# Where four small weight sums stand in VectorE's queue: the first cross product quad of a gate/up stage

## The chip, the cores and the metric

One core of one Trainium2 chip runs the whole program. The metric is the device time of one execution in microseconds; medians of several executions are quoted. Every execution comes with the mean clock that was granted to TensorE (1.0 is full speed).

## The reference

A block of a transformer: layer norm, linear attention with 32 heads, a residual, a second layer norm, a gated ReLU feed-forward layer and a second residual. The change lies in the gate/up part of the feed-forward layer:

```python
# x: 1 x 2048 x 1024 bf16, W_gate and W_up: 1024 x 3584, W_down: 3584 x 1024
gate = jnp.einsum("bsd,df->bsf", x, W_gate)
up   = jnp.einsum("bsd,df->bsf", x, W_up)
gate = gate * (gate > 0)
h    = gate * up
return jnp.einsum("bsf,fd->bsd", h, W_down)
```

## The kernel before

All large products are computed with a fast 2 x 2 block scheme of seven block products, m1 to m7, in place of eight. It needs sums of blocks on both sides. VectorE makes them. One "quad" is one such scheme for 128 gate and 128 up columns of each of the two halves of the feed-forward layer (that is what the seven products combine) and one half of the tokens. Its weight sums (t1 to t4) are made ahead of it by four steps for gate and four for up:

```python
steps = [  # L693, L697, L698, L699; each 128 x 512, 16 bit
    first,                                                    # t1 = b12 - b11
    lambda: tt(out=t2, in0=b22, in1=t1, op=ALU.subtract),     # (shortened)
    lambda: tt(out=t3, in0=b22, in1=b12, op=ALU.subtract),
    lambda: tt(out=t4, in0=b21, in1=t2, op=ALU.subtract),
]
# products 1..7 take the weights  b11, b21, b22, t4, t1, t2, t3
```

The first four quads take one half of the tokens each ("single-token quads"). After them come groups of quads for both halves, and each group opens with a quad that also computes a "cross product", p1 to p7, the same scheme once more on a smaller block. Its weight sums are eight steps (L984, 128 x 256, gate and up in turn for t1, t2, t3, t4). In the names below, g0 to g3 are adds on VectorE with a ReLU on ScalarE behind them, x0 to x3 the products gate times up, j the joins of cross products (VectorE), and c and s copies (ScalarE). The "filling work" is sums for the later down product, with their stores.

In the traces of this case VectorE runs its instructions in the order in which the code emits them: the prediction derives the times of 16 starts from the code, and the changed kernel's trace has them in that order, each 0.1 us earlier. The matmuls of TensorE keep the order of the code too (in the trace of before p1 starts at 326.04, p2 at 326.90, m4 at 327.76, m3 at 330.73, p6 at 332.46, p5 at 333.32, m1 at 334.18, p7 at 335.91, m5 at 336.77, m6 at 338.63), while weight loads run ahead (the first of m6 by 0.34 us in the same trace). Work that is not urgent waits in a list, and `slot(n)` emits a share of it at fixed places between the urgent steps. The end of the last single-token quad, and the filling of the list at the head of each quad:

```python
# in the last single-token quad (r == NE - 1)
now = sums_of_run(r + 1)
steps = [p for pair in zip(*[steps for steps, _ in now]) for p in pair]   # t1 gate, t1 up, t2 gate, ...
work += cross_sums + cross_weight_sums(runs[r + 1][0]) + steps[:2]
held_back = steps[2:]
...
# at the head of every quad
work += held_back + later[:take]
held_back = []
...
if k:
    want = -(-len(fill) // max(nwin - 2 - k, 1))
    for p in range(want):
        work.insert(min(len(work), 2 * p + 1), fill.pop(0))    # filling work goes in between
```

The first cross quad, in order of emission and shortened ("prv" is the last single-token quad, whose final products run into this one):

```python
x["p1"](); x["c1"]()
prv["g3"]()          # VectorE: read accY (m5 + ...) and add: L925
x["p2"](); x["j00"]()
prv["m4"]()
slot(0, 9)
prv["x3"]()
prv["m3"]()          # TensorE: adds onto accY, so g3 must have read it
prv["rg"](); prv["x2"]()
x["p6"](); x["c2"](); x["p5"]()
prv["g1"](); slot(1, 8); prv["x1"]()
cur["m1"](); x["p7"](); x["c3"]()
cur["g0"]()          # VectorE: read accA
slot(2, 4)
cur["m5"](); x["j11"](); slot(3)
cur["m6"]()          # TensorE: adds onto accA; its weights are the t2 sums (L697)
...
```

## Time and profile before

| | before |
|---|---|
| time, median of 3 (lowest to highest) | 729.22 us (729.22 to 730.75) |
| span of the profiled execution | 727.5 us |
| TensorE busy | 719.0 us, 99% |
| VectorE busy | 583.2 us, 80% |
| TensorE's only wait in the gate/up stage (waits view) | 1.1 us, for the add g3 |

The page of a profile gives totals; the waits view gives, for each engine, whom it waited for and for how long; the timeline gives instructions in order of time, like ones merged. The prediction below shows the lines of all of these. One more reading is used throughout: the length of the first cross quad by starts, from its first matmul (p1) to the first matmul of the next quad (m1). A difference of two starts on the same engine doesn't depend on how the profile models the end of a matmul, nor on how late the whole program began.

```profile
326.04 0.59 PE L1004 MATMUL accA<-hn,wg 128*128 128x512 bf16 x2
...
343.81 1.03 PE L916 MATMUL accA<-hn,wg 128*128 128x512 bf16 x4
```

These are the two ends in the timeline of before, so the quad takes 343.81 - 326.04 = 17.77 us.

### The profile page before, as it was taken

To read this page: it belongs to the slowest core of one execution; us is meant where nothing else is said; L and a number is where in the kernel's file an instruction comes from. 1 tells how busy PE (TensorE), PEld (TensorE's weight loads), DVE (VectorE), ACT (ScalarE), POOL (GpSimd) and SP (SyncE) were. 2 spreads that over 40 slices of the span, in tenths; PEclk is the share of its full clock that TensorE was granted. 3 is DMA by queue.
4 is the path that set the end of the run, shared out by engine and by line. 5 is a ranking of instruction groups with operands and counts; after the bars stand their busy time and mean duration, and the time that the engine had idled before them with its cause. 6 is when DMAs were issued, how large, how long until landed. Compare 5 with 4: busy or idle time off the path is not lost.

```text
span 727.5 us, 10634 instructions
## 1 busy us (share of the span) xinstructions
PE 719.0 (99%) x4000; PEld 380.4 (52%) x4000; DVE 583.2 (80%) x1039; ACT 325.2 (45%) x580; POOL 20.8 (3%) x56
## 2 busy tenths in 40 slices
PE   8999999999999999999999999999999999999997
PEld 3454555444444444444444444444444468888666
DVE  6998754777898776889998998988977379996677
ACT  4786653878886564344444444443444120000000
POOL 1000000000000000000000000000000001100210
PEclk9999999999999999999999999999999999999999
DMA  9676003089986533197556585565653499977932
GB/s 318 166 139 174 0 1 115 3 181 232 229 174 170 132 79 109 49 276 210 174 176 195 200 257 202 186 189 179 211 163 128 151 394 313 326 263 261 260 45 59
DMA packets 144708, 128.89 MB, mean 177 GB/s; under 512 B 50960, under 2 KB 127888, under 8 KB 144656
## 3 DMA queue, kind: packets, MB, share of 16 engines
q1 hardware_dynamic: 137584, 123.30, 56.2%
q0 software_dynamic: 5312, 3.15, 3.5%
q10 hardware_dynamic: 1760, 1.77, 0.7%
q8 instruction: 31, 0.51, 0.3%
q14 instruction: 21, 0.17, 0.1%
HBM read 76.81 MB, written 39.85 MB: 160 GB/s over the span
## 4 chain that ended last, share of the span: by engine, by line
PE 92%; DVE 4%; ACT 2%; DMA 1%; issue 0%; SPq 0%; DVEq 0%; ACTq 0%
PE accA L916 21%; PE accA L1410 8%; PE attn L608 7%; PE Aq L365 6%; PE accX L916 6%; PE accY L916 5%; PE accA L1236 3%; PE Aq L789 3%; PE Aq L505 3%; PE accX L1410 3%; PE Eq L365 3%; PE accY L1410 3%; PE accA L1004 2%; PE vp L416 2%; PE kp L398 2%; PE Eq L789 2%
## 5 line engine op out<-in xcount | busy, mean ns | idle before, releaser
L921 ACT COPY snap<-accA 128x1024 f32<-128x1024 f32 x52 | 52.4, 1010 | 65.8 <-PE accA L916 65.6
L926 ACT ACTIVATE gu<-gu 128x512 bf16<-128x512 bf16 x72 | 45.4, 630 | 80.6 <-DVE gu L925 80.5
L916 PEld LDWEIGHTS <-tg 128*128 128x128 f16 x384 | 37.6, 98 | 45.4 <-issue 0.3
L916 PEld LDWEIGHTS <-tu 128*128 128x128 f16 x384 | 37.6, 98 | 45.3
L608 PE MATMUL attn<-wo_mem,oT 128*128 128x512 bf16 x256 | 59.0, 379 | 0.5 <-DVE o_sb L585 0.4
L916 PE MATMUL accA<-hn,tg 128*128 128x512 f16 (+1 forms) x192 | 49.3, 379 | 0.0
L916 PE MATMUL accA<-hn,tu 128*128 128x512 f16 (+1 forms) x192 | 49.3, 379 | 0.0
L205 ACT COPY u<-Aq 128x512 f32<-128x512 f32 x54 | 31.4, 581 | 36.5 <-PE Aq L365 19.7
L1410 PEld LDWEIGHTS <-x 128*128 128x128 f16 (+1 forms) x448 | 43.8, 98 | 5.5
L608 PEld LDWEIGHTS <-oT 128*128 128x128 bf16 x256 | 24.7, 98 | 29.9 <-issue 2.2
L925 DVE TENSOR_TENSOR gu<-accX,snap 128x1024 bf16<-128x1024 f32 x26 | 31.7, 1221 | 10.1 <-ACT snap L921 7.8
L925 DVE TENSOR_TENSOR gu<-accY,snap 128x1024 bf16<-128x1024 f32 x26 | 31.7, 1220 | 7.7 <-ACT snap L921 7.7
L916 PEld LDWEIGHTS <-wg 128*128 128x128 bf16 x208 | 20.3, 98 | 25.8 <-issue 1.4
L916 PEld LDWEIGHTS <-wu 128*128 128x128 bf16 x208 | 20.4, 98 | 24.5
L365 PEld LDWEIGHTS <-xT 128*128 128x128 bf16 (+1 forms) x192 | 18.6, 98 | 21.9 <-issue 0.3
L611 DVE SCALAR_TENSOR_TENSOR x_res<-attn,x_res 128x512 bf16<-128x512 f32 x32 | 22.0, 687 | 9.5 <-PE attn L608 9.3
L1374 POOL DMA_DIRECT2D out_dram<-o x12 | 15.2, 1265 | 502.7 <-DVE o L1370 501.0
L585 DVE TENSOR_TENSOR o_sb<-nd,rd 128x384 bf16<-128x384 f32 (+1 forms) x48 | 23.7, 509 | 7.1 <-ACT rd L584 6.1
L1410 PEld LDWEIGHTS <-xs 128*128 128x128 f16 x280 | 27.4, 98 | 3.2
L1416 DVE TENSOR_TENSOR snap<-accA,u 128x1024 f32<-128x1024 f32 x16 | 19.6, 1222 | 11.4 <-PE accA L1410 11.3
L929 DVE TENSOR_TENSOR hq<-gu 128x512 bf16<-128x512 bf16 x48 | 20.3, 423 | 10.0 <-ACT gu L926 9.8
L1236 PEld LDWEIGHTS <-x 128*128 128x128 bf16 (+1 forms) x168 | 16.4, 98 | 19.6
(268 smaller groups left out, 1516.7 us busy)
## 6 DMA issues: line engine op xcount, KB each, us to landing
x<-x_dram SPq DMA_DIRECT2D x17, 896.0 KB, 8.9
x_dram<-hq SPq DMA_DIRECT2D x28, 512.0 KB, 3.0
wg<-in_B_W_gate_dram SPq DMA_DIRECT2D x14, 512.0 KB, 4.6
wu<-in_B_W_up_dram SPq DMA_DIRECT2D x14, 512.0 KB, 5.8
x_dram<-hq SPq DMA_DIRECT2D x28, 256.0 KB, 2.4
wraw<-in_B_W_down_dram SPq DMA_DIRECT2D x14, 512.0 KB, 4.2
t_dram<-wt SPq DMA_DIRECT2D x21, 256.0 KB, 2.2
xd<-x_dram SPq DMA_DIRECT2D x6, 896.0 KB, 6.6
```

The costliest lines, as they stand in the source:

```text
L205: copies[nm, v] = nc.scalar.copy(out=snaps[nm, v], in_=bank[v][:])
L365: nc.tensor.matmul(ps[:], lhsT=left[m - 1][:, kc, r + v * P:r + (v + 1) * P], rhs=right[m - 1][:, kc, :], start=(start and kc == 0), stop= ...
L585: nc.vector.tensor_tensor(out=ov[:, c0:c0 + n], in0=ndv[:, :, 0:P].rearrange("p k (h e) -> p k h e", h=HPC), in1=rd[:, 0:n, :].unsqueeze(3 ...
L608: nc.tensor.matmul(ps[:], lhsT=st["oT"][:, c, :], rhs=wo_sb[:, c, j * NW:(j + 1) * NW], start=(c == 0), stop=(c == KC - 1))
L611: added[t, j] = nc.vector.scalar_tensor_tensor(out=h_sb[:, j * NW:(j + 1) * NW], in0=ps[:], scalar=1.0, in1=h_sb[:, j * NW:(j + 1) * NW], ...
L789: nc.tensor.matmul(ps[:], lhsT=w(v, m)[:, kc, :], rhs=left[m - 1][:, kc, :], start=(start and kc == 0), stop=(kc == KH - 1), skip_group_ch ...
L916: nc.tensor.matmul(ps[:, v, :], lhsT=w[v][n - 1][:, kc, :], rhs=left[n - 1][:, kc, :], start=(t is not None and kc == 0), stop=(kc == KH - ...
L921: nc.scalar.copy(out=st[nm][:], in_=halves(st["A"]))
L925: add(out=g[:], in0=halves(st[nm]), in1=st[base][:], op=ALU.add)
L926: nc.scalar.activation(out=g[:, 0, :], in_=g[:, 0, :], func=ACT.Relu)
L1236: nc.tensor.matmul(ps[:, t * NW:(t + 1) * NW], lhsT=x_tile(n, s, kh)[:, f, (t0 + t) * P:(t0 + t + 1) * P], rhs=w_tile(n, kh)[:, f, :], sta ...
L1410: nc.tensor.matmul(pv[:, tt, :], lhsT=left(m)[:, f, tt * P:(tt + 1) * P], rhs=right(m)[:, f, :], start=(t is not None and f == 0 and tt % ...
```

## The change

The intent: the cross product's last four weight sums are needed late (t3 for p7, t4 for p4), so they need not stand in front of the urgent add g3. They join the six sums that were already held back for the next quad, ten in all. This is called the first hunk below, though it stands last in the diff. The second hunk sends the filling work of that quad behind the held sums rather than between them.

```diff
-            held_back = []
...
                 for p in range(want):
-                    work.insert(min(len(work), 2 * p + 1), fill.pop(0))
+                    work.insert(len(work) if held_back else min(len(work), 2 * p + 1), fill.pop(0))
+            held_back = []
...
-                    work += cross_sums + cross_weight_sums(runs[r + 1][0]) + steps[:2]
-                    held_back = steps[2:]
+                    cross_steps = cross_weight_sums(runs[r + 1][0])
+                    work += cross_sums + cross_steps[:4] + steps[:2]
+                    held_back = cross_steps[4:] + steps[2:]
```

## The prediction

0.81 us won in front of g3, plus 0.13 us of waiting for g0, less 0.41 us lost anew at m6, came to 0.53 us.

> **What bounds the kernel now.** I read the page first: its header, the busy times and the slices.
>
> ```profile
> span 727.5 us, 10634 instructions
> PE 719.0 (99%) x4000; PEld 380.4 (52%) x4000; DVE 583.2 (80%) x1039; ACT 325.2 (45%) x580; POOL 20.8 (3%) x56
> PE   8999999999999999999999999999999999999997
> PEclk9999999999999999999999999999999999999999
> ```
>
> TensorE is busy for 719.0 of 727.5 us at full clock. No other engine can be the bound, and a change that removes no matmul can win at most 8.5 us, of which most lies at the two ends (the slices marked 8 and 7). Next I asked the waits view of TensorE, which says how much of those 8.5 us is waiting on another engine, and then the busy times by stretch through the stage that the change touches.
>
> ```profile
> PE tp L350 <- DVE xT L351: 1.4, 1, 1.4
> PE spin L451 <- DVE zero L448: 1.2, 1, 1.2
> PE accY L916 <- DVE gu L925: 1.1, 1, 1.1
> PE attn L608 <- DVE o_sb L585: 0.4, 1, 0.4
> ```
> ```profile
> 314.00:326.00 12.00, 12.00 (x57) 5.43 (x56) 10.32 (x20) 5.13 (x8) 0.00 (x0) 1.00 0.95 283
> 326.00:344.00 18.00, 16.92 (x78) 7.53 (x77) 17.30 (x38) 8.73 (x11) 0.00 (x0) 1.00 0.75 225
> 344.00:362.00 18.00, 18.00 (x85) 8.16 (x84) 16.26 (x32) 7.88 (x11) 0.00 (x0) 1.00 0.47 158
> 374.00:392.00 18.00, 18.00 (x85) 8.19 (x84) 14.99 (x28) 9.40 (x12) 0.00 (x0) 1.00 0.96 294
> ```
>
> The columns of the second fence are length, TensorE, weight loads, VectorE, ScalarE, GpSimd, clock, DMA. The stretch 326 to 344 us is the first cross product quad. It alone loses TensorE time (16.92 of 18.00), and there VectorE is busy 17.30 of 18.00 us, 96%. The next cross quad, 374 to 392, loses nothing. So the whole stage from 290 to 560 us has one gap, 1.1 us, and one owner. The timeline shows it (columns: start, duration, engine, line, output<-inputs):
>
> ```profile
> 328.39 0.28 DVE L984 TENSOR_TENSOR ct<-wg,ct 128x256 f16<-128x256 bf16 x1
> 328.59 0.29 DVE L984 TENSOR_TENSOR ct<-wu,ct 128x256 f16<-128x256 bf16 x1
> 328.63 1.03 PE L916 MATMUL accA<-hn,tu 128*128 128x512 bf16 x4
> 328.79 0.42 DVE L693 TENSOR_TENSOR tg<-wg 128x512 f16<-128x512 bf16 x1
> 329.12 0.42 DVE L693 TENSOR_TENSOR tu<-wu 128x512 f16<-128x512 bf16 x1
> 329.46 1.22 DVE L925 TENSOR_TENSOR gu<-accY,snap 128x1024 bf16<-128x1024 f32 x1
> 330.73 1.02 PE L916 MATMUL accY<-hs,wg 128*128 128x512 f16 x4 [1.08 <-DVE gu L925]
> 335.72 0.41 DVE L697 TENSOR_TENSOR tu<-wu,tu 128x512 f16<-128x512 bf16 x1
> 337.36 1.22 DVE L925 TENSOR_TENSOR gu<-accA,snap 128x1024 bf16<-128x1024 f32 x1
> 338.29 0.10 PEld L916 LDWEIGHTS <-tg 128*128 128x128 f16 x1
> 338.63 1.02 PE L916 MATMUL accA<-hs,tg 128*128 128x512 f16 x4
> ```
>
> The matmul at 330.73 is product m3 of the previous quad. It adds onto accY, which the vector add "g3" (L925) must first have read; g3 ran late, from 329.46 to 330.68, because it stood in VectorE's queue behind the weight sums of L984 and L693. Matmuls of this stage start every 0.86/4 = 0.215 us, so m3 could have begun at 328.63 + 0.86 = 329.49 and lost 1.24 us by starts (1.08 by modelled ends). The last lines show a second, small one: product m6 began at 338.63, not at 337.64 + 0.86 = 338.50, because "g0" ended at 338.58. Together 1.37 us by starts; nothing else in this stage is to be won.
>
> [...] 0.20 us for L984 (328.39 to 328.59), 0.33 for L693 (328.79 to 329.12), 1.13 for L925; the recorded durations, 0.29, 0.42 and 1.22, overlap by about 0.09. I use spacings, not durations. [...] m6's first load ran at 338.29, 0.34 us before its held matmul.
>
> **The change part by part.** It removes and adds no instruction; the order of TensorE and of ScalarE is the same, only VectorE's and the DMA queue's differ.
>
> Before, the last single-token quad queued eight sums for the cross product (L984) and two of the next quad's (L693), and six (L697, L698, L699 for gate and up) were held back to the first cross quad. Now the last four L984 sums are held back with those six: ten in the held list, but only four really move. In the new VectorE order these four no longer stand in front of g3: two come after it and after the join L1011, two after "g1". Removed in front of g3: 4 x 0.20 = 0.81 us (measured as the sum of those four spacings: 0.20, 0.20, 0.21, 0.20). The two instructions among them (a multiply and a sum, L929 and L759) move earlier; the multiply's input, a ReLU, was ready at 325.96 + 0.63 = 326.59, so nothing new waits.
>
> So g3 starts at 328.65 and ends at 329.87, and m3 follows 0.05 us later, as now, at 329.92: 0.81 us gained, 0.43 us of the gap kept.
>
> Now VectorE's chain to m6, with the spacings of today: join L1011 329.78; two moved sums 330.91 and 331.11; multiply 331.31; multiply from PSUM 331.65; three sums 332.37, 332.83, 333.17; g1 333.51 to 334.73; two moved sums 334.64 and 334.84; multiply at 335.48 (its ReLU ends at 335.45); sum 335.94; g0 336.28 to 337.50. TensorE wants m6 at 338.50 - 0.81 = 337.69, so g0 no longer holds it. But the moved sums push both L697 sums behind g0, and m6 has these as its weights. Gate's L697 runs 337.42 to 337.84. The wait now sits on the weight load, so 0.05 us for the signal and 0.21 us from load to matmul follow (as between 337.42 and 337.64): m6 at 338.10. That loses 0.41 us anew. Up's L697 ends at 338.17, before its loads at about 338.75.
>
> Sum at m6: 338.63 - 338.10 = 0.53 us. After it nothing should hold TensorE: the last moved sums lie before their products (L984's fourth sum at 335.13, product p4 at 339.82; join L1011 ends 339.96, p3 at 340.68). At 345.06 VectorE idles 0.88 us for a ScalarE copy, which itself follows TensorE, so the queue catches up there and the 0.53 us stay to the end, since later TensorE shows no wait. Predicted span 727.0 us, time 729.22 - 0.53 = 728.7 us.
>
> **The rivals.** First: the wait is wholly replaced, gain nothing, 729.2 us. The unbroken chain on VectorE between 335 and 338 us speaks for it: one more slip of half a microsecond in g1's ReLU or in the L697 sums and m6 gives all back. Against it: g1's and g0's spacings are those of the trace.
>
> Second: the wait at m6 is smaller than I think, because the loads are fetched during the running matmul. Then the gain is up to 0.81 + 0.13 = 0.94 us, 728.3 us. Against it: the load cannot start before its weights are written.
>
> Third: transfers. One filling sum (L759) goes from 332.06 to the end of the quad, about 343.3. Its store therefore leaves at about 343.8 instead of 332.51, and a load into the same buffer, which started at 339.17, must wait for that store to land (4.0 us in this stretch): to about 347.8, and lands about 7 us after, at 355. Its first reader is a vector sum in front of the store that the DMA queue issues at 370.29, so some 14 us remain. Only if that were an earlier reader (one at 350.5) would VectorE stop for several microseconds and TensorE lose perhaps 2 us: 731 us. I read the order of VectorE as showing the later one.
>
> Fourth: VectorE becomes the bound through the stage. The stretch 344 to 362 has it busy 16.26 of 18.00 us, so it has room, and the total of its work is unchanged.
>
> **Range and chances.** The known gap is 1.37 us, 0.19% of the time, so 2% (14.6 us) is out of reach upward, and downward only an unseen stop of many microseconds could do it. The three runs of before read 729.22, 729.22 and 730.75, so runs of one kernel differ by up to 1.5 us, more than the effect. Low end: the full 0.94 us and some luck, 727.5. High end: my 0.53 us on a run like 730.75, 730.3. Faster 0.01, same 0.98, slower 0.01.
>
> **What would show it.** In the waits view the entry accY L916 <- DVE gu L925 falls from 1.1 to about 0.3 us (0.43 by starts), and a new one of 0.2 to 0.4 us appears at accA L916, whose releaser is VectorE's L697, or as a gap in front of the weight load of tg. g3's add starts some 0.8 us nearer to the end of m4's matmuls. The cross quad ends 0.5 us sooner and TensorE's busy time in 326 to 344 rises by as much. I am wrong if g3 is still late (another instruction or a wait takes its place), if m6 loses over 0.9 us, or if a wait for the filling load shows on VectorE near 350 us.

## The result

| | before | changed |
|---|---|---|
| time, median of 6 | 729.43 us | 728.45 us |
| lowest to highest | 729.22 to 730.75 | 728.24 to 730.43 |
| span of the profiled execution | 727.5 us | 726.7 us |
| first cross quad by starts | 17.77 us | 17.03 us |

The ratio of the times is 0.9989, with a 95% interval from 0.9976 to 1.0002. A ratio here is the mean time of one kernel's runs over that of the other's of the same rounds, so it isn't quite the ratio of the medians in the table. The timer alone doesn't separate the two kernels; the trace does.

The waits view of TensorE after the change, against the one in the prediction (the columns are total, times, longest):

```profile
PE tp L350 <- DVE xT L351: 1.4, 1, 1.4
PE spin L451 <- DVE zero L448: 1.2, 1, 1.2
PE attn L608 <- DVE o_sb L585: 0.4, 1, 0.4
PE accY L916 <- DVE gu L925: 0.3, 1, 0.3
```

Nothing moved except the last line, from 1.1 to 0.3 us. The timeline shows both ends of the quad, the add g3 (L925 on accY), the product m3 behind it, and m6 with its weight sum:

```profile
325.96 0.38 PE L1004 MATMUL accA<-hn,wg 128*128 128x512 bf16 x1
...
328.55 1.03 PE L916 MATMUL accA<-hn,tu 128*128 128x512 bf16 x4
328.56 1.21 DVE L925 TENSOR_TENSOR gu<-accY,snap 128x1024 bf16<-128x1024 f32 x1
...
329.83 1.02 PE L916 MATMUL accY<-hs,wg 128*128 128x512 f16 x4 [0.25 <-DVE gu L925]
...
336.73 1.03 PE L916 MATMUL accY<-hs,tu 128*128 128x512 f16 x4
337.32 0.41 DVE L697 TENSOR_TENSOR tg<-wg,tg 128x512 f16<-128x512 bf16 x1
...
337.79 0.55 PEld L916 LDWEIGHTS <-tg 128*128 128x128 f16 x4 [0.53 <-DVE tg L697]
337.80 1.04 PE L916 MATMUL accA<-hs,tg 128*128 128x512 f16 x4
...
342.99 1.03 PE L916 MATMUL accA<-hn,wg 128*128 128x512 bf16 x4
```

g3 starts at the same moment as the last matmuls of m4 (328.56 and 328.55), where before it started 0.83 us after them. m3 could have started at 328.55 + 0.86 = 329.41 and starts at 329.83: 0.42 us are lost where 1.24 us were. m6 could have started at 336.73 + 0.86 = 337.59 and starts at 337.80: 0.21 us are lost, and now the releaser is the L697 sum of gate and the wait sits on the weight load, where before it was 0.13 us for the add g0. Together 0.63 us are left of 1.37. The quad is 17.77 - 17.03 = 0.74 us shorter.

One warning on reading these two profiles. The page of the changed kernel says "PE 716.2 (99%) x3947" where before has 719.0 for 4000 instructions. That isn't 2.8 us of work less: the order of TensorE's instructions is the same in both, and 53 matmul records are missing from the later trace. So busy times of TensorE aren't compared here, only starts.

### The profile page after: what moved, and what is told of

Same layout as the page of the kernel before. It is cut to its first block, busy times and chain, and to the rows that moved or that the text cites. A ratio compares the mean times of both kernels' runs of the same rounds, so it can differ in the third digit from the quotient of the medians.

```text
span 726.7 us, 10581 instructions
## 1 busy us (share of the span) xinstructions
PE 716.2 (99%) x3947; PEld 380.2 (52%) x4000; DVE 582.9 (80%) x1039; ACT 325.4 (45%) x580; POOL 20.8 (3%) x56
## 4 chain that ended last, share of the span: by engine, by line
PE 91%; DVE 4%; ACT 2%; DMA 1%; issue 1%; SPq 0%; DVEq 0%; ACTq 0%
PE accA L916 21%; PE accA L1411 8%; PE attn L608 7%; PE Aq L365 6%; PE accX L916 6%; PE accY L916 5%; PE accA L1237 3%; PE Aq L789 3%; PE Aq L505 3%; PE accX L1411 3%; PE Eq L365 3%; PE accY L1411 3%; PE accA L1004 2%; PE vp L416 2%; PE kp L398 2%; PE Eq L789 2%
## 5 line engine op out<-in xcount | busy, mean ns | idle before, releaser
L925 DVE TENSOR_TENSOR gu<-accX,snap 128x1024 bf16<-128x1024 f32 x26 | 31.7, 1219 | 10.2 <-ACT snap L921 7.8
L925 DVE TENSOR_TENSOR gu<-accY,snap 128x1024 bf16<-128x1024 f32 x26 | 31.7, 1219 | 7.4 <-ACT snap L921 7.4
```

The lines of the kernel that those rows point to most:

```text
L925: add(out=g[:], in0=halves(st[nm]), in1=st[base][:], op=ALU.add)
```

## The experiments

My theory: the quad's length is set by two things in turn. TensorE first waits for g3, which waits for the sums in front of it in VectorE's queue. Later it waits for whichever is last at m6: its own arrival, the add g0, or the chain of VectorE up to gate's L697 sum. A sum that is moved from in front of g3 to a place in front of L697 makes the first wait shorter and leaves the second chain as it was. The main rival: only the start of g3 counts. A second rival: VectorE, 96% busy in this quad, is simply the bound, and any wait that is removed comes back.

Except for the last three, which repeat sums, the experiments change the order of the same instructions on VectorE, and with it when stores and loads are issued, and nothing else. Four of them use a small table of exact slot sizes for this quad:

```diff
+    counts = {}
     def slot(n, parts=0):
-        for _ in range(-(-len(work) // (parts or SLOTS - n))):
+        for _ in range(counts.pop(n, -(-len(work) // (parts or SLOTS - n)))):
             work.pop(0)()
...
             if first:
+                if r == NE:
+                    counts.update({0: 4, 1: 2, 2: 4})      # differs by experiment
```

All kernels gave correct results.

### Two more sums behind g3

```diff
-                    work += cross_sums + cross_steps[:4] + steps[:2]
-                    held_back = cross_steps[4:] + steps[2:]
+                    work += cross_sums + cross_steps[:2] + steps[:2]
+                    held_back = cross_steps[2:] + steps[2:]
```

> The changed kernel, with two more sums (t2 of the cross product) held back until after g3. My theory: the time is set by the later of two things at m6, TensorE's own arrival and VectorE's chain up to the L697 sum of gate. g3 starts 0.40 us earlier than in the changed kernel, so m3 waits 0.0 to 0.05 us and the entry accY L916 <- DVE gu L925 goes; but the two sums lie in front of m6 as well, so gate's L697 stays where it is (337.3 us) and m6 still starts at 337.8: its gap grows from 0.21 to about 0.6 us by starts, and the span stays 726.7 us, the gain over before 0.75 us. Rival (only the start of g3 counts): 0.40 us more, span 726.3, gain 1.15 us. On the load of m6: if a wait on the load costs 0.21 us up to the matmul, as I predicted, matmul starts at 338.0; if not, 0.01 us after the load.

Waits view and timeline of this kernel:

```profile
PE accA L916 <- DVE tg L697: 0.4, 1, 0.4
```
```profile
329.16 1.02 PE L916 MATMUL accY<-hs,wg 128*128 128x512 f16 x4
...
336.06 1.03 PE L916 MATMUL accY<-hs,tu 128*128 128x512 f16 x4
...
337.05 0.41 DVE L697 TENSOR_TENSOR tg<-wg,tg 128x512 f16<-128x512 bf16 x1
...
337.52 0.55 PEld L916 LDWEIGHTS <-tg 128*128 128x128 f16 x4 [0.93 <-DVE tg L697]
337.52 1.04 PE L916 MATMUL accA<-hs,tg 128*128 128x512 f16 x4 [0.44 <-DVE tg L697]
```

The wait for g3 is gone, and a wait of 0.4 us for L697 has taken its place. By starts, m6 loses 337.52 - (336.06 + 0.86) = 0.60 us. The quad takes 17.02 us, as the changed kernel's 17.03. Time 728.33 us (ratio to before 0.9986, from 0.9973 to 0.9999). So the wait for g3 was removed in full, 0.4 us of TensorE's time, and all of it was given back 8 us later. The rival that counts only g3's start falls. The timer couldn't have told this: the difference that the rival expects is 0.40 us, less than the interval.

### The t2 sums of gate and up in front of g0

```diff
-                    held_back = cross_steps[4:] + steps[2:]
+                    held_back = cross_steps[4:6] + steps[2:4] + cross_steps[6:] + steps[4:]
```

> The changed kernel, with gate's and up's L697 sums put right behind g1, into the time in which VectorE waits for a ReLU, and the two t4 sums of the cross product moved behind g0. My theory: m3 keeps its gap (0.25 us in the waits view, 0.42 by starts); g0 ends at about 337.4 as now and m6 starts at TensorE's own pace, 337.59 instead of 337.80: 0.21 us more gained, span 726.5 us, gain over before 0.95 us. Rival (only the start of g3 counts): span 726.7 us, unchanged, and the gap at m6 only takes another form.

m6 starts 0.87 us after the second half of m5 (337.45 and 336.58), which is TensorE's own pace; m3 keeps its wait of 0.25 us in the timeline (0.2 in the waits view). The quad takes 16.82 us, 0.95 us less than before and 0.21 less than the changed kernel. Time 728.22 us (ratio 0.9985, from 0.9973 to 0.9997). The two sums cost nothing in their new place, because VectorE stood still there for the ReLU between g1 and its product: that product starts 1.98 us after g1 here (335.24 and 333.26) and 1.97 us in the changed kernel (335.39 and 333.42).

### Half of the move

```diff
-                    work += cross_sums + cross_steps[:4] + steps[:2]
-                    held_back = cross_steps[4:] + steps[2:]
+                    work += cross_sums + cross_steps[:6] + steps[:2]
+                    held_back = cross_steps[6:] + steps[2:]
```

> The changed kernel with half of the move: only the two t4 sums of the cross product are held back, the two t3 sums stand in front of g3 again. My theory (the later of two things): g3 0.40 us later than in the changed kernel, m3 at about 330.23, but L697 of gate is ready at 337.8 as before and TensorE itself reaches m6 only at 337.99: no gap at m6. Gain over before 0.56 us, that is three quarters of the full gain for half of the move; span 726.9 us. Rival (gain in proportion to the moved sums): half, 0.37 us, span 727.1 us.

m3 starts at 330.10, 0.82 us after it could; m6 starts at 337.87, 0.87 us after the second half of m5 at 337.00, so without a wait. The quad takes 17.22 us: 0.55 us gained for half of the move, against 0.74 for the whole. Time 728.54 us (ratio 0.9992, from 0.9980 to 1.0003). The gain isn't proportional to what is moved; the second half of the move earns only 0.19 us, since from there on the L697 chain is the later of the two.

### Only the first hunk, and only the second

The changed kernel with the old place of the filling work:

```diff
-                    work.insert(len(work) if held_back else min(len(work), 2 * p + 1), fill.pop(0))
+                    work.insert(min(len(work), 2 * p + 1), fill.pop(0))
```

> The changed kernel with only its second hunk undone: the filling sums go among the held sums again instead of behind them. My theory: g3 and m3 stay as in the changed kernel (gap 0.25 us in the waits view), but the filling items take places in the slots, and gate's L697 comes after both t4 sums of the cross product and up's L697 after the join L1011. m6's gate half then starts at about 338.3 instead of 337.8 and its up half at about 339.8: some 1.1 us lost against the changed kernel, 0.4 us slower than before; span about 727.8 us, time about 729.6 us. Rival (only the start of g3 counts): as the changed kernel, span 726.7 us, time 728.5 us.

```profile
PE accA L916 <- DVE tg L697: 0.6, 1, 0.6
PE accA L916 <- DVE tu L697: 0.4, 1, 0.4
...
PE accY L916 <- DVE gu L925: 0.3, 1, 0.3
```

The wait for g3 is as short as in the changed kernel, yet the quad takes 18.18 us, 0.41 us longer than before: both halves of m6 now wait for their L697 sums. Time 729.46 us against 729.22 (ratio 1.0003, from 0.9989 to 1.0017). Without its second hunk the change would have gained nothing.

The kernel before with only the new place of the filling work:

```diff
-            held_back = []
...
                 for p in range(want):
-                    work.insert(min(len(work), 2 * p + 1), fill.pop(0))
+                    work.insert(len(work) if held_back else min(len(work), 2 * p + 1), fill.pop(0))
+            held_back = []
```

> The kernel before with only the second hunk of the change: the filling sum L759 goes to the end of the quad, the four sums of the cross product stay in front of g3. My theory: nothing in front of g3 changes, m3's gap stays 1.08 us; g1 and g0 keep their times, since g1's ReLU ends too late anyway (336.5), so m6 stays too: no gain, span 727.5 us, within 0.1 us. Rival (the freed 0.33 us of VectorE reach TensorE): 0.13 us gain at m6.

The quad takes 17.77 us (326.30 to 344.07), exactly as before, and m3's wait is 1.1 us. Time 729.36 us against 729.22 (ratio 1.0001, from 0.9988 to 1.0013). The span of its profiled execution, 727.8 us, is 0.3 us longer than expected; that lies before this quad, which starts at 326.30 instead of 326.04. What cost it there isn't shown. TensorE waited 2.8 us for its first transposed tile instead of 1.4, but it waited 2.6 us in the kernel of the next section too, whose quad starts at 325.90. Alone, the second hunk does nothing. It is worth 18.18 - 17.03 = 1.15 us with the first, because it keeps the filling work from pushing L697 behind m6's arrival.

### Both waits removed

The two edits of the first two experiments together, and the product x1 behind g0:

```diff
-                    work += cross_sums + cross_steps[:4] + steps[:2]
-                    held_back = cross_steps[4:] + steps[2:]
+                    work += cross_sums + cross_steps[:2] + steps[:2]
+                    held_back = cross_steps[2:6] + steps[2:4] + cross_steps[6:] + steps[4:]
...
                 slot(1, 8)
-                prv["x1"]()
+                if r > NE:
+                    prv["x1"]()
...
                 cur["g0"]()
+                if r == NE:
+                    prv["x1"]()
                 slot(2, 4)
```

> The two edits late_t2 and early697 together, and the product that follows g1 (x1) put behind g0, so that g0 starts at 335.2 instead of 336.2 us. My theory: m3 at 329.43 and m6 at 337.2 with no wait; no TensorE gap is left between 326 and 344 us (busy 18.0 of 18.0), gain over before 1.36 us, 0.61 us over the changed kernel: span 726.1 us, time about 727.9 us. Rival (a new wait takes the place, at p4, p3 or m7, because VectorE is the bound of this quad): some 0.75 us as in the changed kernel, 728.5 us.

The ends of the quad in the timeline:

```profile
325.90 0.38 PE L1004 MATMUL accA<-hn,wg 128*128 128x512 bf16 x1
...
342.31 1.03 PE L916 MATMUL accA<-hn,wg 128*128 128x512 bf16 x4
```

The waits view of TensorE has no line of the gate/up stage any more. The quad takes 342.31 - 325.90 = 16.41 us, 1.36 us less than before, which is the whole of the 1.37 us that the prediction counted as lost. Time 727.75 us against 729.22 (ratio 0.9982, from 0.9970 to 0.9994); four of its five executions read 727.74 to 727.77, the fifth 729.68 at a mean clock of 0.997. This version beats the kernel before by 0.2%; against the changed kernel, which wasn't timed in the same rounds, its quad is 0.62 us shorter. VectorE wasn't the bound of the quad: it is busy there for 17.07 of 17.77 us before (96%) and for 16.27 of 16.41 us here (99%), and in this order TensorE has no wait. The second rival falls, but hardly any room is left, and one filling sum (0.33 us) fewer lies within the quad, since it now runs after it. The busy figure in the expectation (18.0 of 18.0) can't be checked, for the missing records.

### The same cost many times over

To see the cost of a sum in front of g3 above the noise of the timer, the kernel before repeats the four sums that the change moves (same results) right before g3, four more times:

```diff
                 slot(5)
+                if r == NE - 1:
+                    for p in cross_weight_sums(runs[r + 1][0])[4:] * 4:
+                        p()
             assert not work
```

> The kernel before with the four sums that the change moves done five times in all in front of g3 (sixteen more instructions, same results). My theory: sixteen times 0.20 us, so g3 starts 3.25 us later, m3's gap in the waits view grows from 1.08 to 4.3 us, and nothing catches up: span about 730.8 us, time about 732.6 us, 0.45% slower. Rival (a delay of g3 is partly taken up by room behind it, such as the 0.88 us for which VectorE idles near 345 us): less than 2.6 us slower.

```profile
334.34 1.86 PE L916 MATMUL accY<-hs,wg 128*128 128x512 f16 x4 [4.31 <-DVE gu L925]
...
336.00 1.91 PE L916 MATMUL accY<-hs,wu 128*128 128x512 f16 x4
...
337.71 1.87 PE L1004 MATMUL accA<-cs,ct 128*128 128x512 f16 x4
...
339.42 1.03 PE L1004 MATMUL accX<-cs,ct 128*128 128x512 f16 x4
```

The wait is 4.3 us as expected, but the kernel is 5.6 us slower, not 3.25: 734.85 us against 729.22 (ratio 1.0074, from 1.0062 to 1.0087). The expectation missed. The groups of four matmuls behind the wait start 1.66 to 1.71 us apart instead of 0.86: for 339.42 - 334.34 = 5.08 us TensorE ran at half pace, and twelve matmuls took 2.49 us more than 12 x 0.216. The sum fits: g3 came 3.23 us later, plus 2.49, less m6's old loss of 0.13, is 5.59; the quad grew from 17.77 to 349.78 - 326.42 = 23.36 us, by 5.59. In the page of this run the granted clock reads 8 tenths instead of 9 in the one slice that holds most of this quad. Asked by tenths of a microsecond (`prof sixteen --windows`), the trace shows a clock of 0.50 from 332.58 to 339.41 us, for 6.83 us: it fell while TensorE was still waiting. (The one window from 326 to 344 us reads 0.81 on average, which makes 18 x 0.19 / 0.50 = 6.84 us at 0.50.) In all five executions the mean clock is below full, 0.994 to 0.998.

Two smaller doses ask whether this lost clock grows with the wait or sets in at some length. The edits are the same with `* 2` (eight more sums) and `* 3` (twelve).

> The kernel before with the four sums done three times in all in front of g3 (eight more instructions), half of the dose that cost 5.6 us instead of the expected 3.25 us, because TensorE's granted clock fell behind a wait of 4.3 us. Theory A (0.20 us for each sum in front of g3[...]): m3's wait 2.7 us, matmuls behind it at full pace (0.215 us apart), 1.6 us slower than before: span about 729.1 us, time about 730.9 us. Rival B (the clock falls in proportion to the wait): half the 5.6 us, 2.8 us, time about 732.0 us.

> The same with twelve more instructions: m3's wait 3.5 us by modelled ends, 3.7 by starts[...]. Theory A: some executions at full pace (2.4 us slower than before, 731.6 us), some with matmuls at half pace[...], so a wide scatter. Rival B: 4.2 us in every run, 733.4 us.

Timelines of the two, eight sums first:

```profile
332.21 1.02 PE L916 MATMUL accY<-hs,wg 128*128 128x512 f16 x4 [2.68 <-DVE gu L925]
...
333.07 1.03 PE L916 MATMUL accY<-hs,wu 128*128 128x512 f16 x4
```
```profile
333.61 1.86 PE L916 MATMUL accY<-hs,wg 128*128 128x512 f16 x4 [3.48 <-DVE gu L925]
...
335.26 1.54 PE L916 MATMUL accY<-hs,wu 128*128 128x512 f16 x4
...
336.64 1.03 PE L1004 MATMUL accA<-cs,ct 128*128 128x512 f16 x4
```

With eight, matmuls run at full pace behind the wait and the quad takes 345.29 - 325.92 = 19.37 us, 1.60 us more, which is 8 x 0.20. With twelve, the eight matmuls behind the wait took 336.64 - 333.61 = 3.03 us in place of 8 x 0.216 = 1.73; the clock was 0.50 from 332.88 to 336.29 us (asked in the same way), for 3.41 us, half of the stretch with sixteen. The quad grew by 3.58 us, of which 2.41 are the sums and 1.30 the pace, less 0.13 at m6.

| extra sums | executions at mean clock 1.0 | executions at lower mean clock |
|---|---|---|
| 8 | 730.60, 730.76, 730.77 us | 732.12 (0.998), 732.25 (0.997), 734.03 (0.995) |
| 12 | 731.55, 731.62 us | 733.07 (0.998), 733.35 (0.998), 734.51 (0.995) |
| 16 | none | 733.27 (0.998), 734.45 (0.998), 734.85 (0.994), 735.27 (0.994), 735.53 (0.995) |

The executions at full clock follow the count: against the median of before in the same rounds, 729.33 us, they are 1.3 to 1.4 us slower with eight and 2.2 to 2.3 with twelve, 0.16 to 0.19 us for each sum; the trace says 0.20. The loss of clock is a separate thing that strikes some executions and not others, so rival B, a loss in proportion in every run, falls. Theory A was right on the sums; its term for the onset was longer than what the traces show. In the two traces the clock fell 2.7 us (twelve) and 2.5 us (sixteen) after the modelled end of the last matmul, and three of six executions with a wait of 2.7 us had a lower clock too. Where in those three the clock fell isn't known, as one execution of each kernel was traced, here one at full clock. Their size fits the two traces: the one with a single stretch of 3.41 us has a mean clock of 0.998, the one with twice that 0.994, and half clock for 3.41 us costs at most 1.7 us (an estimate, half of it). With eight and twelve sums the executions at 0.997 and 0.998 are 1.4 to 1.8 us longer than those at full clock, the ones at 0.995 2.9 to 3.3 us. Executions of this kind, at 0.997 or 0.998 and some 2 us longer, also turned up among the kernels with short waits or none (731.34 of before, 730.43 of the changed kernel, 730.46 of half the move, 729.68 of the best one), so not all of them can come from this wait.

## Why the prediction was right

**The bound.** TensorE with one loss of 1.1 us in the stage: right. Emptying that loss and its small follower gave 1.36 us, and nothing else in the stage gave or took time.

**The move in front of g3.** Predicted 4 x 0.20 = 0.81 us off g3's start; measured 329.46 - 328.56 = 0.90, of which 0.08 is that the whole stage ran earlier in the second trace (m4's last matmuls at 328.55 instead of 328.63): 0.82. The rest of m3's loss was predicted at 0.43 us and measured at 0.42.

**The new wait at m6.** Its place and its releaser, the weight load of tg held for L697, were predicted and seen. Its size was the one term that was mis-sized: 0.41 us predicted, 0.21 measured. The sum had added 0.21 us from the load to its matmul, read from loads that ran while another matmul was still busy. Behind a wait the matmul starts 0.01 us after its load (337.79 and 337.80), though the load itself lasts 0.10 us, and in the experiment with the longer wait at the same instant (337.52 both). In both traces the matmul starts before its load is over. So the gain was 0.74 us by starts and not 0.53. The prediction's second rival had named the direction, a smaller wait at m6, though for another reason.

**The rivals.** Nothing was wholly replaced: m6 lost 0.21 us, not the 0.9 that would have cancelled the gain. The late filling sum's store left at 343.71 and the load behind it at 345.86 (predicted: 343.8 and 347.8; the store landed in 2.1 us, not 4.0), and no wait on VectorE came of it. VectorE didn't become the bound.

**Range and class.** 728.45 us lies within 727.5 to 730.3, and the class is "same", for the reason given: only 1.37 us were there to be had. That the time fell in this range proves little by itself: the range also held the first rival, no gain at all (729.2 us), and runs of one kernel differ by more than the gain. What bears the mechanism out is the place and the size of the waits in the trace.

## What to carry to other kernels

When TensorE is full, read its few waits by starts, find what stands in front of the releaser in its queue, and then follow the same queue to the next product that depends on it: an instruction that is only moved back may delay that one instead, and the gain is set by the later of the two (here two more sums behind g3 took away a wait of 0.4 us and gave it back at m6). Look for the places where the helper engine itself waits for something else; here two sums of 0.33 us put there cost nothing. An effect of a tenth of a per cent is settled by the trace and by repeated doses of the cost, and a dose that is too large can bring in a second effect, here the clock (0.50 for 6.83 us with sixteen sums), which has to be counted apart.

## What these traces show of the clock, of weight loads and of VectorE

- TensorE's clock: the two stretches at a clock of 0.50 lasted 3.41 us (twelve sums) and 6.83 us (sixteen), one and two times 3.41, and matmuls in them were 0.42 us apart in place of 0.215. The clock fell 2.7 and 2.5 us after the last matmul's modelled end (3.1 and 2.9 us after its start), before the waits of 3.5 and 4.3 us were over. With a wait of 2.7 us, three of six executions had a lower mean clock (0.995 to 0.998) and were 1.4 to 3.3 us longer than the mean of the other three; whether that wait was the cause stays open. With a wait of 3.5 us, two of five kept the full clock.
- Weight loads: a matmul released through its weight load started 0.00 to 0.01 us after the load's start (the changed kernel and late_t2), against 0.21 us in a full stream, where the trace shows no wait of the load (336.52 and 336.73 in the changed kernel).
- VectorE: the add from PSUM (L925) takes 1.13 to 1.14 us from start to start and has a recorded duration of 1.21 to 1.22 us. The sums from SBUF take 0.20 us (L984, 256 elements) and 0.33 us (L693, 512) from start to start, with recorded durations of 0.28 to 0.29 and 0.41 to 0.43 us.
- VectorE at 96% busy cost TensorE 1.37 us in one order, and at 99% in another order it cost nothing: here the order of its queue mattered more than its share of busy time.
